# Attention on one core: a new order of score matmuls with seven shared PSUM banks, and value columns split by query halves

## The chip, the cores and the metric

The kernel runs on 1 core of one Trainium2 chip. The metric is the device time of one execution in microseconds, and lower is better. A core has five engines that work at the same time: TensorE (PE, with its weight loads shown as PEld), VectorE (DVE), ScalarE (ACT), GpSimd (POOL), and SyncE (SP), which issues the transfers. PE writes to PSUM alone, which has eight banks of 128 partitions by 512 fp32 values. DVE and ACT read results out of it. GpSimd works on SBUF.

## The reference

There are four layers over a sequence of 2048 rows of width 576. Layers 1 and 3 (called A) are attention with 32 heads of 18 columns, layers 2 and 4 (called B) have one key and value head for all 32 query heads.

```python
def _A_ref(x, wqkv, wo):
    ...
    scores = jnp.einsum("bhqd,bhkd->bhqk", q, k) * (Dh ** -0.5)
    p = _softmax(scores, axis=-1)
    o = jnp.einsum("bhqk,bhkd->bhqd", p, v)
    ...
x = x + _A_ref(_layernorm(x, axis=-1), A_wqkv, A_wo)
x = x + _B_ref(_layernorm(x, axis=-1), B_wq, B_wk, B_wv, B_wo)
x = x + _A_ref(_layernorm(x, axis=-1), A_wqkv, A_wo)
x = x + _B_ref(_layernorm(x, axis=-1), B_wq, B_wk, B_wv, B_wo)
```

Everything is fp32. Softmax takes the maximum of each row of scores, the exponentials of scores less that maximum, and their sum.

## The kernel before

A layer has a stretch of projections (layer norm, transposes, queries, keys and values) and then its attention. The output projection of a layer runs into the projections of the next. Attention is cut into 64 **units**: 16 pairs of heads (`p`) by 4 blocks of 512 queries (`u`). The loop over units is at line 908.

In a unit three kinds of work are mixed.

- **Maxima** (`max_mm`, line 581). Queries stand on PSUM's partitions and keys in columns: 16 score tiles of 128 queries by 512 keys for each head `a` of the pair. PE computes a tile (L613), DVE takes the maximum of each row (L620). When 32 are done, `max_final` (L759) folds them, GpSimd splits the result in two parts (`hl`), DVE transposes it (L768), and it goes through DRAM into two rows of `big`. From then on a matmul with the queries subtracts the maximum by itself. Maxima run 14 steps ahead of the exponentials, and a unit has 8 steps.
- **Exponentials** (`exp_mm`, line 776). Keys stand on partitions and queries in columns: 16 tiles of 128 keys by 512 queries for each head. PE computes the tile (L782), ACT writes its exponential to a tile `pt` (L791); every fifth goes to a slot of the tile `side` instead.
- **Value columns** (`pv_block`, line 804). PE multiplies values, 18 columns and one of ones, by the exponentials, and adds up in the one bank `oacc` (L812). Four matmuls stand side by side on PE, each on its own 32 of oacc's partitions: two heads by even and odd chunks of 128 keys. So a unit has 8 blocks of 512 columns, each four matmuls wide, and at its end ACT copies oacc to a slot of `side` (L200, called at line 818). `o_sum` (line 821) adds the odd half to the even one on GpSimd, two copies of 32x512 and an addition. Then the row of sums goes through DRAM to be inverted (`l_part`, `l_inv`, `l_out`, `l_rows`), GpSimd multiplies by it (`o_mul`), and `o_out` stores the block. Value columns lag 1152 columns behind (`LAG`).

Score tiles of the two heads go in pairs: one takes the upper half of PE's rows and the other the lower, so both run at once.

A **shared pair** of maxima moves work from DVE to ACT. For two key blocks of the same queries, a tile `d` (L605) is the score of the difference of the two key blocks; ACT takes its relu (L610) to a slot of `side`. The tile `t` (L613) is the score of the second block, and one DVE instruction (L617) adds the relu and takes the maximum. Since max(a, b) = b + relu(a - b), DVE has one pass for two tiles.

The order of a unit is written out in the table `UNIT` (line 67). Each word is one pair of score tiles, a letter for each head: `e` an exponential, `m` a maximum, `d` and `t` the halves of a shared pair. A number after a word says how many value columns follow. PE goes through the words and numbers as they stand. The other engines read tiles in the order in which PE wrote them. A unit before has 4 `d` and 4 `t`, 24 `m` and 32 `e`.

PSUM's eight banks are oacc, three banks for `m` and `t` (`mtile`, line 186) and four for `e` and `d` (`etile`, line 189), each set taken in turn.

The table `UNIT` is used by units 0 to 61 of a layer. In the last two no maxima are left or few, and `ENDS` and `LAST` take its place.

## Time and profile before

| | |
|---|---|
| median of 3 runs | 5597.66 us |
| lowest and highest | 5596.14 and 5599.7 us |
| span of the profiled execution | 5596.1 us |
| its own time | 5596.14 us, the lowest of the three |
| PE, DVE, ACT, POOL busy | 5580.9, 4941.3, 4934.9, 1755.0 us |
| granted TensorE clock, mean | 0.999 |

The profile is one execution. A page gives busy time by engine, the chain of work that ended last, and groups of instructions by line, with their count, their busy time, the mean length of one in ns, and the idle time of the engine before them with what ended it. The times of single instructions come from the timeline, and busy time in a stretch from the view by stretch. Matmuls overlap, and so do instructions of DVE and ACT that follow each other: the rate of an engine is read from the distance between starts and not from the length of one. An fp32 matmul of value columns is recorded as two, so four matmuls side by side are eight records.

### The profile page before, as it was taken

The page shows a single profiled execution, that of the slowest core. Times are in us where ns is not written, and L with a number is a line of the kernel's source. Part 1 is how long each engine was busy: PE and PEld are TensorE (multiplying, and loading weights), DVE is VectorE, ACT ScalarE, POOL GpSimd, SP SyncE. Part 2 cuts the span into 40 slices and gives each one's busy share as a digit, 9 for nine tenths or more (in the row PEclk, how much of TensorE's full clock was granted, in tenths as well). Part 3 has the DMA queues.
Part 4 walks back from the last instruction along what each step waited for, and adds up shares of the span by engine and source line. Part 5 has one row for each costly group of instructions (what it writes and reads, how often), then busy time and mean ns, then how long its engine had stood idle before and what let it go on. Part 6 is the DMA issues. An engine that isn't in the chain of part 4 may idle for free.

```text
span 5596.1 us, 137398 instructions
## 1 busy us (share of the span) xinstructions
PE 5580.9 (100%) x53372; PEld 2836.4 (51%) x53372; DVE 4941.3 (88%) x9504; ACT 4934.9 (88%) x9884; POOL 1755.0 (31%) x2245
## 2 busy tenths in 40 slices
PE   9999999999999999999999999999999999999999
PEld 8644444444844444444686444444448444444446
DVE  5799999998699999999747999999977999999995
ACT  3599999999299999999626999999992999999996
POOL 3133333334233323333421433333342333333332
PEclk9999999999999999999999999999999999999999
DMA  7311111111420110101253111111114201010002
GB/s 238 109 51 35 40 36 40 36 38 29 131 63 24 24 24 21 24 20 25 61 197 97 49 40 35 39 37 37 37 34 137 53 24 24 24 24 20 24 14 80
DMA packets 259573, 293.56 MB, mean 52 GB/s; under 512 B 133724, under 2 KB 173916, under 8 KB 249200
## 3 DMA queue, kind: packets, MB, share of 16 engines
q1 hardware_dynamic: 258920, 284.78, 18.0%
q8 instruction: 419, 6.86, 0.5%
q14 instruction: 234, 1.92, 0.1%
HBM read 158.77 MB, written 121.95 MB: 50 GB/s over the span
## 4 chain that ended last, share of the span: by engine, by line
PE 99%; DVE 1%; ACT 0%; DMA 0%; issue 0%; POOL 0%; SPq 0%; ACTq 0%; POOLq 0%
PE oacc L812 39%; PE pse L782 23%; PE psm L613 21%; PE psn L280 6%; PE psq L439 6%; PE psd L605 3%; PE ps L272 0%; DVE mx L620 0%; PE oacc L273 0%; POOL big L229 0%; DVE ev L456 0%; DMA raw<-in_A_wqkv_dram 0%; DMA kd<-kd_d 0%; ACT ev L447 0%; ACT evr L453 0%
## 5 line engine op out<-in xcount | busy, mean ns | idle before, releaser
L620 DVE TENSOR_REDUCE mxd<-psm 128x1 f32<-128x512 f32 x5952 | 3746.8, 682 | 181.0 <-PE psd L605 66.3
L791 ACT ACTIVATE pt<-pse 128x512 f32<-128x512 f32 x6584 | 3573.3, 627 | 26.1 <-PE pse L782 1.2
L613 PE MATMUL psm<-big 62*128 62x512 f32 x7200 | 2505.5, 444 | 0.7
L782 PE MATMUL pse<-big 64*128 64x512 f32 x8192 | 2415.3, 431 | 1.5 <-ACT evr L453 1.5
L812 PE MATMUL oacc<-pt,vbuf 128*19 128x192 f32 (+6 forms) x20244 | 1795.2, 379 | 0.0
L782 PEld LDWEIGHTS pse<-big 64*128 64x128 f32 x8192 | 1212.9, 184 | 890.9 <-ACT pt L791 513.9
L613 PEld LDWEIGHTS psm<-big 62*128 62x128 f32 x7200 | 1132.8, 184 | 677.2 <-DVE mxd L620 259.6
L812 PE MATMUL oacc<-side,vbuf 128*19 128x64 f32 (+6 forms) x5004 | 1402.3, 377 | 0.0
L791 ACT ACTIVATE side<-pse 128x512 f32<-128x512 f32 x1608 | 995.4, 619 | 5.9
L202 POOL TENSOR_SCALAR hl<-neg 128x8 fp32r<-128x8 f32 x256 | 50.9, 199 | 2446.1 <-DVE neg L759 2446.1
L812 PEld LDWEIGHTS oacc<-pt,vbuf 128*19 128x19 f32 x20244 | 447.8, 97 | 601.6 <-issue 485.2
L617 DVE CUSTOM_DVE_ANT_0 side<-psm,side 128x512 f32<-128x512 f32 x992 | 679.6, 685 | 37.5 <-PE psm L613 14.0
L835 POOL TENSOR_TENSOR rl<-lt,mone 128x8 f32<-128x8 f32 x256 | 423.5, 1654 | 662.0 <-DMA lt<-os 653.9
L610 ACT ACTIVATE side<-psd 128x512 f32<-128x512 f32 x992 | 598.1, 644 | 3.5 <-PE psd L605 3.5
L812 PE MATMUL oacc<-pt,vy 128*19 128x384 f32 (+2 forms) x5700 | 587.2, 417 | 0.0
L812 PE MATMUL oacc<-side,vy 128*19 128x384 f32 (+2 forms) x1404 | 455.6, 415 | 0.0
L605 PE MATMUL psd<-kd,big 54*128 54x512 f32 x992 | 428.4, 473 | 0.8 <-DMA kd<-kd_d 0.8
L812 PEld LDWEIGHTS oacc<-side,vbuf 128*19 128x19 f32 x5004 | 317.3, 97 | 147.0 <-issue 119.5
L447 ACT ACTIVATE ev<-psq 128x512 fp32r<-128x512 f32 (+1 forms) x112 | 67.0, 598 | 315.8 <-PE psq L439 274.2
L848 POOL TENSOR_TENSOR os<-os,rb 96x512 f32<-96x512 f32 x256 | 328.7, 1284 | 21.6 <-DMA rb<-r_d 21.6
L826 POOL TENSOR_TENSOR os<-os,side 96x512 f32<-96x512 f32 x240 | 307.5, 1281 | 20.0
L202 POOL TENSOR_SCALAR os<-side 32x512 f32<-32x512 f32 x480 | 294.5, 614 | 40.1 <-POOL hl L763 0.4
(93 smaller groups left out, 3314.2 us busy)
## 6 DMA issues: line engine op xcount, KB each, us to landing
big<-qk_d SPq DMA_DIRECT2D x180, 432.0 KB
qk_d<-ev SPq DMA_DIRECT2D x96, 512.0 KB
qk_d<-ev SPq DMA_DIRECT2D x120, 256.0 KB
rb<-r_d SPq DMA_DIRECT2D x512, 36.0 KB
o_d<-os SPq DMA_DIRECT2D x512, 36.0 KB
o<-o_d SPq DMA_DIRECT2D x64, 256.0 KB
big<-m_d SPq DMA_DIRECT2D x512, 4.0 KB
lt<-os SPq DMA_DIRECT2D x512, 2.0 KB
```

Source lines behind the costliest of these rows:

```text
L202: eng.tensor_scalar(dst, src, 1.0, 0.0, op0=OP.mult, op1=OP.add)
L280: nc.tensor.matmul(ps, lhs[:, xc, :], wsm[:, wc, h * 288:(h + 1) * 288], start=i == 0, stop=i == len(TERMS) - 1)
L439: nc.tensor.matmul(ps[:n].rearrange("p (u t) -> p u t", u=2)[:, us], w[:, wc, :n], xts[T][:, us, xc, :], start=(xc, wc) == TERMS[0], stop= ...
L605: nc.tensor.matmul(ps, q[b:b + 3 * DH, c0:c0 + P], kds[p if is_a else 0][b:b + 3 * DH], start=True, stop=True)
L610: nc.scalar.activation(r, ps, AF.Relu)
L613: nc.tensor.matmul(ps, q[b:b + KM, c0:c0 + P], k[b:b + KM, kb * 512:(kb + 1) * 512], start=True, stop=True)
L617: nc.vector.tensor_tensor_reduce(out=r, in0=ps, in1=r, scale=1.0, scalar=-3.0e38, op0=OP.add, op1=OP.max, accum_out=mx[:, r0:r0 + 1])
L620: nc.vector.reduce_max(mx[:, r0:r0 + 1], ps, axis=AX.X)
L782: nc.tensor.matmul(e, k[r:r + KE, kc * P:(kc + 1) * P], q[r:r + KE, u * 512:(u + 1) * 512], start=True, stop=True)
L791: nc.scalar.activation(pt, e, AF.Exp, scale=SCALE)
L812: nc.tensor.matmul(oacc[j:j + DH + 1, cs], v_of(kc)[:, 2 * p + a if is_a else 0, :], pts[p, u, i][:, cs], start=kc < 2 and c0 == 0, stop=k ...
L835: nc.gpsimd.tensor_tensor(rl, lts.pop((p, u)), mone, op=OP.pow)
```

## The change

It has four parts.

1. A new table `UNIT`: 11 groups of value columns in place of 12, and three shared pairs a unit in place of four (3 `d`, 3 `t`, 26 `m`, 32 `e`). The cut for the last units moves with it (`CUT_AT`).
2. Seven banks for all score tiles. A second table `BANKS` says for each tile which bank it takes, as a rank by age: 0 is the bank that was taken longest ago, 2 the third oldest. Outside of the units the sets of four and three stay.
3. The four matmuls side by side are now two heads by two halves of the 512 queries, over the same chunk of keys. A unit's value work is 16 blocks of 256 columns, and oacc uses 256 columns of its bank. oacc is copied out as 128x256, GpSimd copies that on to `sums` instead of adding halves, and multiplies 128x256. The transfers of `l_part`, `l_rows` and `o_out` are four in place of two, each half as long.
4. `pt` tiles have 17 buffers in place of 15, and four slots of `side` in place of three take exponentials.

```diff
-UNIT = """te ee 256 em me 384 et em me 512 et me ee 448 md dm em 384 em me 192 me ee me 192 md em 384
-          me me em 384 em ee te 192 mm ee 384 dm em em 384 me"""
+UNIT = """ee 384 em ee mm 384 em mm ee 384 me te ee 512 me me em 320 em me 192 me ed dm 448 em em me
+          320 me em te 256 ee de mt 512 em mm ee 384 em mm"""
+
+BANKS = """01 00 02 01 00 00 10 00 02 20 01 01 10 00 01 00
+           00 01 01 00 01 00 00 01 01 00 01 00 02 01 00 02"""
-CUT_AT = 10
+CUT_AT = 9
...
+    order = list(range(7))
+    turns = {"e": [0, 1, 2, 3], "m": [4, 5, 6]}
+
+    def bank(b, name):
+        order.remove(b)
+        order.append(b)
+        return psum.tile([P, 512], F32, tag=f"b{b}", bufs=1, name=name)
+
+    def oldest(rank):
+        return lambda name: bank(order[rank], name)
...
-        return pool.tile(list(shape), dt, tag="p", bufs=15, name=name)
+        return pool.tile(list(shape), dt, tag="p", bufs=17, name=name)
...
-                n, c0 = divmod(pv_at[0], 512)
-                w = min(cols, 512 - c0)
+                n, c0 = divmod(pv_at[0], 256)
+                w = min(cols, 256 - c0)
...
-            for i in range(i, i + 4) if turn[0] % 2 else range(i + 3, i - 1, -1):
-                a, kc = (i // 2) % 2, i // 4 * 2 + i % 2
-                j = 64 * a + 32 * (kc % 2)
-                nc.tensor.matmul(oacc[j:j + DH + 1, cs], v_of(kc)[:, 2 * p + a if is_a else 0, :], pts[p, u, i][:, cs],
-                                 start=kc < 2 and c0 == 0, stop=kc >= 14 and c1 == 512)
+            for i in range(4) if turn[0] % 2 else range(3, -1, -1):
+                a, h = divmod(i, 2)
+                nc.tensor.matmul(oacc[32 * i:32 * i + DH + 1, c0:c1], v_of(kc)[:, 2 * p + a if is_a else 0, :],
+                                 pts[p, u, a, kc][:, 256 * h + c0:256 * h + c1],
+                                 start=kc == 0 and c0 == 0, stop=kc == NCH - 1 and c1 == 256)
...
+                    copy(nc.scalar if m_done[0] < 4 * ns else nc.vector, oc, oacc[:, :256])
...
-            for j in (0, 64):
-                copy(nc.gpsimd, t[j:j + 32], oc[j + 32:j + 64])
-            nc.gpsimd.tensor_tensor(t[:96], t[:96], oc[:96], op=OP.add)
+            copy(nc.gpsimd, sums[u % 2], ocs.pop((p, u)))
...
-            for a in range(2):
-                nc.sync.dma_start(lt[64 * a:64 * a + 64, :], sums[u % 2][64 * a + DH:64 * a + DH + 1, :])
+            for i in range(4):
+                nc.sync.dma_start(lt[32 * i:32 * i + 32, :], sums[u % 2][32 * i + DH:32 * i + DH + 1, :])
...
+                    take = oldest(BANKS[i][a] if more_m or m_done[0] < 4 * ns else 0)
                     if kinds[a] == "e":
-                        exp_mm(p, u, n // 2 * 4 + 2 * a + n % 2, mtile if m_done[0] == 4 * ns and n_e % 7 % 2 else etile)
+                        exp_mm(p, u, a, e_next[a], take)
```

What this makes of PE's order is seen about the end of a unit's value columns, where oacc is copied out (the third group of a table ends there), in the first layer. Before, PE has these rows; `oacc` are value columns, `pse` tiles for exponentials and `psm` tiles for maxima:

```order
L812 MATMUL oacc<-side,vy 19x512
L812 MATMUL oacc<-pt,vy 19x512 x3
L782 MATMUL pse<-big 128x512
L613 MATMUL psm<-big 128x512 x2
L782 MATMUL pse<-big 128x512 x3
L812 MATMUL oacc<-pt,vbuf 19x448 x4
```

And after the change, at the same place:

```order
L829 MATMUL oacc<-pt,vy 19x128 x2
L829 MATMUL oacc<-side,vy 19x128 x2
L829 MATMUL oacc<-pt,vy 19x256 x4
L633 MATMUL psm<-big 128x512
L801 MATMUL pse<-big 128x512
L633 MATMUL psm<-big 128x512
L801 MATMUL pse<-big 128x512 x3
L829 MATMUL oacc<-side,vbuf 19x256 x2
L829 MATMUL oacc<-pt,vbuf 19x256 x6
```

A value group is now cut at every 256 columns, so 384 columns are 128 and 256, and 512 are two pieces; three pairs of score tiles stand between groups here in both.

DVE's rows of a whole unit before, from the end of one set of maxima (`neg`) to the next; L617 is the sum and maximum of a shared pair, recorded as two instructions, and L768 the transpose:

```order
L620 TENSOR_REDUCE mxd_97<-psm 128x1 x6
L768 STREAM_TRANSPOSE tr<-hl_102 128x32
L620 TENSOR_REDUCE mxd_97<-psm 128x1 x7
L617 ISA side,mxd_97<-psm,side 128x512
L617 ISA mxd_97 128x1
L620 TENSOR_REDUCE mxd_97<-psm 128x1 x6
L617 ISA side,mxd_97<-psm,side 128x512
L617 ISA mxd_97 128x1
L620 TENSOR_REDUCE mxd_97<-psm 128x1 x2
```

And after:

```order
L640 TENSOR_REDUCE mxd_99<-psm 128x1 x4
L788 STREAM_TRANSPOSE tr<-hl_102 128x32
L640 TENSOR_REDUCE mxd_99<-psm 128x1 x8
L637 ISA side,mxd_99<-psm,side 128x512
L637 ISA mxd_99 128x1
L640 TENSOR_REDUCE mxd_99<-psm 128x1
L637 ISA side,mxd_99<-psm,side 128x512
L637 ISA mxd_99 128x1
L640 TENSOR_REDUCE mxd_99<-psm 128x1 x13
```

The rows before are cut where two more L617 and three more reductions follow; after, one more L617 follows and the set ends. The transpose stands four reductions behind `neg` and not six.

More of the change, by code (lines that the diff above doesn't have):

```diff
@@ L86 @@
 UNIT, LAST = slots(UNIT), slots(LAST)
+BANKS = [[int(x) for x in w] for w in BANKS.split()]
+assert len(BANKS) == len(UNIT)
 KINDS = [[w[a] for w, _ in UNIT if w[a] != "e"] for a in range(2)]
@@ L172, in tile_kernel @@
     kd_d = dram.tile([D, 3, 512], F32, name="kd_d")
-    rb = cst.tile([P, 512], F32, name="rb")
+    rb = cst.tile([P, 256], F32, name="rb")
+    sums = [cst.tile([P, 256], F32, name=f"os{i}") for i in range(2)]
     mxd = [cst.tile([P, 32], F32, name=f"mxd{i}") for i in range(2)]
@@ L177, in tile_kernel, with turn_of @@
         nc.gpsimd.memset(t, -3.0e38)
[L179 removed]
     hls = [cst.tile([P, 32], F32R, name=f"hl{i}") for i in range(2)]
[L182 removed]
+    for t in [rb] + [h_.bitcast(F32) for h_ in hls]:
         nc.gpsimd.memset(t, 0.0)
+    order = list(range(7))
[6 more added lines that the diff above has]
+        return lambda name: bank(order[rank], name)
+    def turn_of(kind, name):
+        b = turns[kind].pop(0)
+        turns[kind].append(b)
+        return bank(b, name)
     def mtile(name):
[L187 removed]
+        return turn_of("m", name)
     def etile(name):
[L190 removed]
+        return turn_of("e", name)
     def ptile(name, shape=(P, 512), dt=F32):
[L193 removed]
+        return pool.tile(list(shape), dt, tag="p", bufs=17, name=name)
     def xtile(name, shape=(P, 2, 9, 256), dt=F32R):
@@ L603, in max_mm @@
             if kind == "d":
-                ps = etile("psd")
+                ps = tile("psd")
                 nc.tensor.matmul(ps, q[b:b + 3 * DH, c0:c0 + P], kds[p if is_a else 0][b:b + 3 * DH],
```

52 lines of the change are left out of this document (22 added, 30 removed).

## The prediction

> **What bounds the kernel now.** First the page: which engine is full, and what its chain of waits ends in.
>
> ```profile
> PE 5580.9 (100%) x53372; PEld 2836.4 (51%) x53372; DVE 4941.3 (88%) x9504; ACT 4934.9 (88%) x9884; POOL 1755.0 (31%) x2245
> PE 99%; DVE 1%; ACT 0%; DMA 0%; issue 0%; POOL 0%; SPq 0%; ACTq 0%; POOLq 0%
> ```
>
> PE is named for all the span. But matmuls overlap in these rows, so a wait of some 0.1 us can't be seen in busy time. Hence the view by stretch, over a stretch of the first layer, with the groups of instructions of the same stretch (of ACT's copies out of oacc and of DVE's rows).
>
> ```profile
> 401.88:1297.60 895.72, 895.72 (x9216) 403.62 (x9216) 852.68 (x1633) 889.80 (x1776) 285.50 (x352) 1.00 0.15 37
> L200 ACT ACTIVATE side<-oacc 128x512 f32<-128x512 f32 x48 | 28.7, 598 | 0.0
> L620 DVE TENSOR_REDUCE mxd<-psm 128x1 f32<-128x512 f32 x1153 | 726.0, 682 | 34.1 <-PE psd L605 11.4 <-PE psm L613 9.4 <-PE pse L782 4.2
> L617 DVE CUSTOM_DVE_ANT_0 side<-psm,side 128x512 f32<-128x512 f32 x192 | 131.5, 685 | 7.3 <-PE psm L613 2.5 <-PE pse L782 0.2
> ```
>
> The columns of the first row are length, then busy time of PE, PEld, DVE, ACT and POOL. oacc is copied out once a unit, so 48 units took 895.72 us: 18.66 us a unit, at a granted clock of 1.00. Of this DVE shows 17.76 busy and ACT 18.54. To see what PE needs, I read its timeline in one unit (start, length, line).
>
> ```profile
> 402.12 0.72 PE L613 MATMUL psm<-big 62*128 62x512 f32 x2
> 402.46 0.63 PE L782 MATMUL pse<-big 64*128 64x512 f32 x3
> 403.01 0.95 PE L812 MATMUL oacc<-pt,vbuf 128*19 128x448 f32 x8
> 403.89 0.49 PE L613 MATMUL psm<-big 62*128 62x512 f32 x1
> ...
> 404.87 0.56 PE L812 MATMUL oacc<-pt,vbuf 128*19 128x64 f32 x9
> ...
> 405.64 0.49 PE L782 MATMUL pse<-big 64*128 64x512 f32 x1
> ...
> 406.30 0.34 PE L812 MATMUL oacc<-pt,vbuf 128*19 128x192 f32 x1
> ...
> 406.75 0.50 PE L613 MATMUL psm<-big 62*128 62x512 f32 x1
> ...
> 407.80 0.35 PE L812 MATMUL oacc<-pt,vbuf 128*19 128x192 f32 x2
> ...
> 409.69 0.50 PE L613 MATMUL psm<-big 62*128 62x512 f32 x1
> ...
> 410.59 0.50 PE L812 MATMUL oacc<-pt,vbuf 128*19 128x384 f32 x1
> ...
> 411.36 0.50 PE L782 MATMUL pse<-big 64*128 64x512 f32 x1
> ```
>
> PE alternates between score pairs and a group of value columns. Three pairs last 0.89 (402.12 to 403.01) or 0.90 (409.69 to 410.59), two pairs 0.66 (405.64 to 406.30): a third pair adds 0.24, so opening a group is dear. 448 value columns last 0.88 (403.01 to 403.89), 192 last 0.45 (406.30 to 406.75): 1.68 ns a column and 0.13 to get back to scores. The old table has 12 groups, eight of three pairs and four of two: 8 x 0.90 + 4 x 0.66 + 12 x 0.13 + 4096 x 0.00168 = 7.20 + 2.64 + 1.56 + 6.88 = 18.28 us. The unit took 18.66, so PE waits 0.38 us a unit, in places such as 403.89 to 404.87 (0.98 for three pairs) and 406.75 to 407.80 (1.05). What it waits for, in the view of waits for this stretch:
>
> ```profile
> PEld pse L782 <- ACT pt L791: 91.2, 154, 0.8
> PEld psm L613 <- DVE mxd L620: 49.0, 144, 0.6
> ```
>
> These are waits for a bank to be read out; most lie under running matmuls. The other two engines have their own floors:
>
> ```profile
> 404.42 3.68 DVE L620 TENSOR_REDUCE mxd<-psm 128x1 f32<-128x512 f32 x6 [0.22 <-PE psd L605]
> 408.02 0.20 DVE L768 STREAM_TRANSPOSE tr<-hl 128x32 f32<-128x32 f32 x1
> 408.15 4.56 DVE L620 TENSOR_REDUCE mxd<-psm 128x1 f32<-128x512 f32 x7
> 412.62 0.68 DVE L617 CUSTOM_DVE_ANT_0 side<-psm,side 128x512 f32<-128x512 f32 x1
> ...
> 413.31 1.29 DVE L620 TENSOR_REDUCE mxd<-psm 128x1 f32<-128x512 f32 x2
> ...
> 421.35 0.69 DVE L617 CUSTOM_DVE_ANT_0 side<-psm,side 128x512 f32<-128x512 f32 x1
> ...
> 421.96 0.69 DVE L620 TENSOR_REDUCE mxd<-psm 128x1 f32<-128x512 f32 x1
> 422.68 0.19 DVE L759 TENSOR_REDUCE neg<-mxd 128x8 f32<-128x32 f32 x1
> 402.31 0.60 ACT L200 ACTIVATE side<-oacc 128x512 f32<-128x512 f32 x1
> 402.81 0.59 ACT L791 ACTIVATE pt<-pse 128x512 f32<-128x512 f32 x1
> 412.87 2.07 ACT L791 ACTIVATE pt<-pse 128x512 f32<-128x512 f32 x4
> 414.78 0.65 ACT L610 ACTIVATE side<-psd 128x512 f32<-128x512 f32 x1
> ```
>
> A reduction behind another costs DVE 0.60 (404.42 to 408.02, six). A sum-and-maximum of a shared pair (L617) costs 0.61 (421.35 to 421.96) to 0.69 (412.62 to 413.31), say 0.65. Transpose and final maximum add 0.13 (408.02 to 408.15) and about 0.31 (421.96 to 422.68 in place of 0.60, and 0.19). So DVE needs 24 x 0.60 + 4 x 0.65 + 0.44 = 17.44 us a unit. ACT needs 0.48 an exponential or relu (412.87 to 414.78, four), and 0.50 for the copy of oacc: 36 x 0.48 + 0.50 = 17.78. PE is the bound by 0.5, and the other two are close.
>
> By the Trainium skill (Perfetto Trace Analysis, "Identifying the Most-Contended Engine") the occupancy of Vector and Scalar is a fair measure of how near they are to their limit, by which ACT with 99.3% would be the bound. This trace speaks against it: ACT's rows overlap, 0.6 long but 0.48 apart.
>
> **The change, part by part.** *Fewer switches on PE.* The new table has 11 groups, ten of three pairs and one of two, and the same 32 pairs and 4096 columns: 10 x 0.90 + 0.66 + 11 x 0.13 + 6.88 = 17.97. That is 0.31 us a unit less.
>
> *Blocks of 256 columns.* Cut at every 256, a unit's value work falls into 20 pieces in place of 16. 384 columns in one piece last 0.77 (410.59 to 411.36), in pieces of 64 and 320 also 0.77 (404.87 to 405.64): a piece costs nothing to the 0.01 that these rows resolve, so 0 to 0.04 us a unit; I take 0. That the two halves of a query block stream out of the same tile has no row of its own; the two maxima at 402.12 read one tile, big, side by side and lose nothing, so 0 again.
>
> The far bound is that a matmul's fixed part is not hidden. In the same stretch, 64 and 128 columns:
>
> ```profile
> L812 PE MATMUL oacc<-pt,vbuf 128*19 128x64 f32 x920 | 43.4, 224 | 0.0
> L812 PE MATMUL oacc<-pt,vy 128*19 128x128 f32 x922 | 49.4, 275 | 0.0
> ```
>
> 64 columns more cost 51 ns, so 224 - 51 = 173 ns of a record don't depend on columns. A piece is two passes of four matmuls side by side; bare, four more pieces would cost 4 x 2 x 0.173 = 1.38 us a unit. The two rows of 0.77 say that it is hidden.
>
> The Trainium skill (TensorEngine Tiling (Array Packing), "Instruction Overhead") speaks against this part: each matmul carries an overhead of about 60 cycles, and a dimension that is small already shouldn't be cut. With the 2.4 GHz that the skill gives for TensorE (Trainium Kernel Development and Optimization, "NeuronCore Architecture") an estimate is 25 ns for each of 4 x 2 passes, 0.2 us a unit, or four times that if the four matmuls of a pass queue; the unit would be 18.5 to 19.1. This trace does not show such a cost at 64 columns.
>
> *Three shared pairs.* A shared pair is two maxima for one relu on ACT and one pass on DVE. One pair fewer: ACT loses a relu, 0.48. DVE has 26 reductions and 3 sums in place of 24 and 4, 2 x 0.60 - 0.65 = 0.55 more: 17.99 a unit. DVE's floor is now as high as PE's.
>
> *Copy of half a bank.* ACT copies 256 columns of oacc, not 512. No row has that copy from PSUM; it saves at least nothing and at most the 0.50; I take 0.25, by the half. ACT then needs 17.78 - 0.48 - 0.25 = 17.05 and drops out as a bound.
>
> *GpSimd.* The add of two halves goes: two copies of 32x512 and the add become one copy. POOL has time to spare, and only the lt chain waits on it:
>
> ```profile
> 407.49 1.29 POOL L848 TENSOR_TENSOR os<-os,rb 96x512 f32<-96x512 f32 x1
> 411.46 1.65 POOL L835 TENSOR_TENSOR rl<-lt,mone 128x8 f32<-128x8 f32 x1 [2.68 <-DMA lt<-os]
> 422.96 0.20 POOL L202 TENSOR_SCALAR hl<-neg 128x8 fp32r<-128x8 f32 x1 [9.85 <-DVE neg L759]
> ```
>
> POOL stands idle 9.85 us before the next unit's hl, so this is worth 0; without that cover the 1.3 us of a copy or product would delay hl, and with it DVE's transpose four reductions (2.4 us) behind. The three steps over SP (lt, rb, o_d) issue four transfers each, not two: six more a unit in SP's queue, ahead of the rows for later units. Waiting for POOL they hold SP no longer than now, since POOL's copy is shorter; DMA is busy 0.15 of this stretch; 0.
>
> *Seven banks by rank.* This is the term with no row. Now each maximum's matmul has to wait until all but two of DVE's earlier tiles are read, each exponential's and relu's until all but three of ACT's are. Counted through the new ranks, of the 29 banks that a unit takes over from DVE, 18 allow three or four tiles behind, ten allow two and one allows one; of the 35 from ACT, 6 allow four, 17 three and 12 two. So DVE may carry about one tile (0.60 us) more over a long value group, which is where it runs dry. On the other hand a late DVE now also holds up exponentials. Bounds: the waits vanish, and the unit is DVE's 17.99; or DVE keeps the idle time it has before its rows now, (34.1 + 7.3) / 48 = 0.86, and the unit is 18.85. The nearest row is PE's own wait of 0.38 over its floor; with both floors at 17.97 and 17.99 and a deeper queue I take 0.35: a unit of 18.32.
>
> *Sum.* 18.32 - 18.66 = -0.34 us a unit, times 62 units a layer that use the table, times 4: -84 us. The last two units of a layer are bound by exponentials alone and projections are untouched: 0. The two more pt buffers can free at most small waits of the projections, 0 taken. The profiled execution has a span of 5596.1 us, which is also the fastest time of the three; from the median 5597.66 the sum gives 5513 us.
>
> **Rivals.**
> *DVE runs dry* (slower). With 29 passes DVE has only 18.66 - 17.99 = 0.67 us of idle time a unit before the kernel is slower than now. Place: the two value groups of 512 and the one of 448, where DVE gets two tiles (1.2 us) for 1.8 to 1.9 us of PE work. For it: the 0.86 of idle time now. At 18.85 a unit: +0.19 x 248 = +47, 5645 us. Against it: ranks that allow three behind.
> *Order gives it back.* The banks' ranks tie ACT's and DVE's tiles together, and waits grow by the 0.31 that was saved: within 11 us of now, 5598.
> *Waits vanish.* DVE's 17.99 holds: -0.67 x 248 = -166, 5432 us.
> *Short matmuls cost* (slower from a point on). If a quarter of the 1.38 us is bare, 0.34, the gain is gone, 5598; all of it gives 5513 + 1.38 x 248 = 5855 us. The rows of 0.77 are against it. The tiling page's overhead, above, would be this rival's mechanism.
> *That PE's saving isn't real* (the third pair no cheaper in the new groups) is part of the second.
>
> **How the numbers follow.** Chances: forecast (unit 18.2 to 18.5, so 5484 to 5558) 0.58; waits vanish 0.10; between forecast and no change 0.05; no change 0.07; DVE runs dry 0.17; short matmuls past zero 0.03. So faster by over 0.2% (11 us, about what a measurement of this kernel can tell from no change) 0.73, same 0.07, slower 0.20. The range leaves out the far end of both outer rivals: 5440 to 5625.
>
> **What would show it.** Right: about 18.3 us a unit between copies of oacc, three pairs still 0.90 to value columns, 256-wide pieces at 0.43 each, DVE's idle time before its reductions under 0.4 a unit, ACT's share down by some 0.7 us a unit. Wrong: PE's three pairs at 1.0 or more in most groups (banks), DVE rows with idle time behind the groups of 448 and 512 columns (dry), or value groups longer than 1.68 ns a column (pieces).

## The result and the profile after

The changed kernel takes 5567.22 us (median of 4 runs, 5565.1 to 5567.69) against 5597.17 for the kernel before (4 runs beside it, 5596.14 to 5599.7): a ratio of 0.9945, with a 95% interval of 0.993 to 0.9959. It is faster by 30 us. The forecast was 84 us faster. The direction was right, and the size was off by more than half.

First the page: its busy times, and the row of the chain by engine.

```profile
PE 5542.7 (100%) x61788; PEld 3174.4 (57%) x61788; DVE 4992.7 (90%) x9504; ACT 4806.7 (86%) x9636; POOL 1070.9 (19%) x1731
PE 22%; ACT 1%; DVE 0%; issue 0%; ACTq 0%
```

PE is still full in this view; ACT has lost 2 points of the span and DVE gained 2. The chain by engine adds up to 23% of the span here, where before it covered all of it, so nothing is read from it. Then the same stretch of the first layer as in the prediction, by stretch and by group (columns as there), and the first and the last of the copies out of oacc in it, from ACT's timeline (start, length, line).

```profile
401.88:1297.60 895.72, 895.72 (x10848) 471.08 (x10852) 871.56 (x1647) 872.76 (x1744) 159.59 (x260) 1.00 0.15 38
L640 DVE TENSOR_REDUCE mxd<-psm 128x1 f32<-128x512 f32 x1259 | 773.5, 682 | 22.5 <-PE psm L633 18.2 <-PE pse L801 3.1
L810 ACT ACTIVATE pt<-pse 128x512 f32<-128x512 f32 x1239 | 674.7, 614 | 19.4 <-PE psm L633 6.9 <-PE pse L801 2.1 <-ACT pt L810 0.4
L220 ACT ACTIVATE side<-oacc 128x256 f32<-128x256 f32 x49 | 19.4, 395 | 0.1
```
```profile
402.09 0.40 ACT L220 ACTIVATE side<-oacc 128x256 f32<-128x256 f32 x1
...
1290.34 0.40 ACT L220 ACTIVATE side<-oacc 128x256 f32<-128x256 f32 x1
```

49 copies are 48 units: (1290.34 - 402.09) / 48 = 18.51 us a unit, where 18.32 was forecast and 18.66 was measured before. 0.15 us times 248 units is 37 us, of which 30 arrive. ACT's rows of these copies in all four layers show the rest: from the first to the last one of a layer, 59 units, the four layers together save 35.5 us, and what lies outside of these stretches is 4.5 us longer (1193.2 us against 1188.7).

PE's timeline in a unit after the change, in the part that turned out to matter:

```profile
406.37 0.50 PE L633 MATMUL psm<-big 62*128 62x512 f32 x1
...
407.40 0.40 PE L829 MATMUL oacc<-pt,vbuf 128*19 128x256 f32 x2
...
408.27 0.49 PE L801 MATMUL pse<-big 64*128 64x512 f32 x1
...
408.84 0.40 PE L801 MATMUL pse<-big 64*128 64x512 f32 x1
409.17 0.51 PE L829 MATMUL oacc<-pt,vbuf 128*19 128x64 f32 x10
...
409.84 0.50 PE L633 MATMUL psm<-big 62*128 62x512 f32 x1
409.84 0.73 PE L801 MATMUL pse<-big 64*128 64x512 f32 x2
410.18 0.63 PE L633 MATMUL psm<-big 62*128 62x512 f32 x2
410.53 0.50 PE L801 MATMUL pse<-big 64*128 64x512 f32 x1
410.95 0.63 PE L829 MATMUL oacc<-pt,vbuf 128*19 128x256 f32 x8
411.51 0.50 PE L801 MATMUL pse<-big 64*128 64x512 f32 x2
```

Three pairs that wait for nothing last 0.90 (408.27 to 409.17), as before. Ahead of the group of 448 they last 1.03 (406.37 to 407.40), and ahead of the group of 256 columns 1.11 (409.84 to 410.95). In the second case the last tile of the third pair, an exponential, starts late, at 410.53. What it waited for is seen on ACT's timeline at that place, in a stretch that holds one instruction:

```profile
409.82 0.66 ACT L810 ACTIVATE pt<-pse 128x512 f32<-128x512 f32 x1
```

It ends at 409.82 + 0.66 = 410.48, and PE starts 0.05 later. The tile that took the bank before was one of ACT's.

Since `BANKS` fixes which tile had a bank before, this can be followed for every tile: the start of its matmul in PE's timeline against the end of the instruction that last read its bank. Over 47 units from 401.88 on, the late tile ahead of the group of 256 starts 0.05 behind the end of an instruction of ACT in all 47, and the last tile ahead of the group of 448 does so in 41. Where the first group of 384 is late in this way (14 units), the bank is ACT's too. In none of these cases had another of the seven banks come free earlier, so no other rank would have shortened these waits at their places.

Over the 48 units the three pairs ahead of the group of 256 last 0.24 more than 0.90, and those ahead of the group of 448 last 0.09 more (means of the timeline's starts over this stretch; the other waits in this text are worked out the same way). Two groups of 384 have 0.07 and 0.05, and the groups of 512 have 0.03 and 0.02. Together with small rests this is 0.55 us of waits a unit (the unit of 18.51 less PE's floor of 17.96, see below; with 0.90 and 0.66 taken off for the pairs it is 0.53), where the forecast had 0.35. By the same count the old order has 0.41.

The view of waits says something else. It names DVE for most of PE's waiting:

```profile
PEld pse L801 <- DVE mxd L640: 84.4, 232, 0.4
PEld psm L633 <- DVE mxd L640: 58.9, 164, 0.4
PEld pse L801 <- ACT pt L810: 18.9, 101, 0.3
```

Most of this lies under running matmuls, and an entry goes to the semaphore that came last. So who sets the unit was left to experiments.

### The profile page after: what moved, and what is told of

It is laid out like the page before. It is cut to its first block, busy times and chain, and to the rows that moved or that the text cites. A ratio compares the mean times of both kernels' runs of the same rounds, so it can differ in the third digit from the quotient of the medians.

```text
span 5565.1 us, 157695 instructions
## 1 busy us (share of the span) xinstructions
PE 5542.7 (100%) x61788; PEld 3174.4 (57%) x61788; DVE 4992.7 (90%) x9504; ACT 4806.7 (86%) x9636; POOL 1070.9 (19%) x1731
## 5 line engine op out<-in xcount | busy, mean ns | idle before, releaser
L640 DVE TENSOR_REDUCE mxd<-psm 128x1 f32<-128x512 f32 x6448 | 3961.0, 682 | 117.5 <-PE psm L633 95.7
L633 PE MATMUL psm<-big 62*128 62x512 f32 x7448 | 2255.5, 434 | 1.3 <-ACT pt L810 0.5
L829 PE MATMUL oacc<-pt,vbuf 128*19 128x256 f32 (+2 forms) x24544 | 1742.6, 341 | 0.0
L801 PEld LDWEIGHTS pse<-big 64*128 64x128 f32 x8192 | 1188.7, 184 | 714.4 <-DVE mxd L640 425.5
L829 PEld LDWEIGHTS oacc<-pt,vbuf 128*19 128x19 f32 x24544 | 628.1, 98 | 659.0 <-issue 428.6
L829 PE MATMUL oacc<-side,vbuf 128*19 128x256 f32 (+3 forms) x6016 | 774.1, 341 | 0.0
L829 PE MATMUL oacc<-pt,vy 128*19 128x256 f32 (+1 forms) x8192 | 564.8, 341 | 0.0
L829 PEld LDWEIGHTS oacc<-pt,vy 128*19 128x19 f32 x8192 | 225.4, 98 | 194.5 <-issue 134.1
L829 PE MATMUL oacc<-side,vy 128*19 128x256 f32 (+1 forms) x2016 | 263.0, 339 | 0.0
L300 PE MATMUL psn<-wsm,ot 128*128 128x288 f32 x1792 | 244.8, 296 | 0.4
L300 PEld LDWEIGHTS psn<-wsm,ot 128*128 128x128 f32 x1792 | 238.6, 188 | 5.5 <-issue 3.0
```

Of the source, the lines that this page charges most:

```text
L300: nc.tensor.matmul(ps, lhs[:, xc, :], wsm[:, wc, h * 288:(h + 1) * 288], start=i == 0, stop=i == len(TERMS) - 1)
L633: nc.tensor.matmul(ps, q[b:b + KM, c0:c0 + P], k[b:b + KM, kb * 512:(kb + 1) * 512], start=True, stop=True)
L640: nc.vector.reduce_max(mx[:, r0:r0 + 1], ps, axis=AX.X)
L801: nc.tensor.matmul(e, k[r:r + KE, kc * P:(kc + 1) * P], q[r:r + KE, u * 512:(u + 1) * 512], start=True, stop=True)
L829: nc.tensor.matmul(oacc[32 * i:32 * i + DH + 1, c0:c1], v_of(kc)[:, 2 * p + a if is_a else 0, :], pts[p, u, a, kc][:, 256 * h + c0:256 * h ...
```

## The experiments

Five theories were tested. **D**: DVE, whose floor rose to 17.99, sets the unit. **B**: the order in which banks are given out does. **A**: ACT does, because the banks that it reads come free late. **P**: PE itself needs that long for a third pair. **S**, a form of A that came up later: ACT's sum over a unit counts, wherever its work stands. "A unit" below is the mean of 56 units in the middle of the first layer. Ratios are to the kernel before.

**d1: shorter maxima.** DVE gets relief and nobody else. The reductions of the units that share the banks read 448 of 512 keys; the kernel leaves the other 64 out of these maxima.

```diff
-                    nc.vector.reduce_max(mx[:, r0:r0 + 1], ps, axis=AX.X)
+                    nc.vector.reduce_max(mx[:, r0:r0 + 1], ps[:, :448] if shared else ps, axis=AX.X)
```

> The changed kernel, whose reductions of plain maxima read 448 of 512 columns (64 columns are left out of those maxima). Theory D (DVE sets the unit: its floor of 17.9 to 18.0 us and two places a unit where it runs dry make 18.51): with 26 reductions some 0.06 us shorter DVE's floor falls by about 1.6 us, DVE no longer binds, and the unit falls to PE's floor plus small waits, 18.0 to 18.2 us, 5470 to 5490 us in all. Theory B (the shared banks' ranks tie exponentials to banks, whatever DVE's speed): the unit stays at 18.4 to 18.5, 5545 to 5567 us.

5566.03 us, 0.9946 (0.9934 to 0.9959), a unit of 18.50: no change, as was expected of theory B. The stretch and DVE's group in it:

```profile
401.88:1297.60 895.72, 895.72 (x10852) 472.31 (x10850) 805.21 (x1647) 872.97 (x1745) 159.67 (x260) 1.00 0.15 38
L640 DVE TENSOR_REDUCE mxd<-psm 128x1 f32<-128x448 f32 x1259 | 706.7, 617 | 88.7 <-PE psm L633 61.7 <-PE pse L801 23.4
```

DVE's busy time fell from 871.56 to 805.21, and all of it became idle time of DVE (22.5 to 88.7). The waits of PE stayed at the same places. Theory D falls.

**k0 and k1: other ways to give out banks.** k0 sets every rank to 0, so that each tile takes the bank that was taken longest ago. k1 keeps the new table with the old split of four banks and three.

```diff
-BANKS = """01 00 02 01 00 00 10 00 02 20 01 01 10 00 01 00
-           00 01 01 00 01 00 00 01 01 00 01 00 02 01 00 02"""
+BANKS = "00 " * 32
```
```diff
-                    take = oldest(BANKS[i][a] if more_m or m_done[0] < 4 * ns else 0)
+                    own = "m" if kinds[a] in "mt" else "e"
+                    take = (lambda name, own=own: turn_of(own, name)) if more_m or m_done[0] < 4 * ns else oldest(0)
```

> The changed kernel with every rank 0, so that each score tile takes the bank that was taken longest ago. Theory D: the number of banks counts and the ranks hardly, 0 to +25 us against the changed kernel (5567 to 5592). Theory B: the ranks matter, over 30 us either way.

> The changed kernel with the old split of banks in the units: three in turn for m and t, four in turn for e and d. Theory D: DVE may then carry only two tiles behind, runs dry longer behind the groups of 448 and 512 columns, and the unit goes to 18.8 to 19.0 us, 70 to 120 us over the changed kernel (5637 to 5687). Theory B: exponentials no longer wait for banks that DVE holds, and the kernel gets faster, below 5550 us.

k0: 6016.19 us, 1.0749 (1.0734 to 1.0764), a unit of 20.31. k1: 5896.0 us, 1.0535 (1.052 to 1.0549), a unit of 19.82. The new table needs its ranks; without them it would have lost 5 to 7%. Other ways to give out the banks cost 1.3 to 1.8 us a unit, far outside of what the prediction had as bounds for this term. k0 meets what was expected of theory B, k1 meets neither expectation. At the late tiles of k0 the bank that is taken is in no unit the first to come free: another had been free for 0.34 to 0.90 us in the mean, place by place. In the changed kernel the late tiles already take the first bank to come free, so wrong ranks there are not what its 0.55 comes from; whether a wholly other table of ranks would do better, no run shows.

**p1 and s1: the parts without the new table.** p1 is the kernel before with the value columns by query halves, the half copy, GpSimd's single copy, four transfers and 17 buffers, in the old order and with split banks; its edit on the kernel before, cut to its core:

```diff
-                n, c0 = divmod(pv_at[0], 512)
+                n, c0 = divmod(pv_at[0], 256)
...
-                copy(nc.scalar if m_done[0] < 4 * ns else nc.vector, oc, oacc)
+                    copy(nc.scalar if m_done[0] < 4 * ns else nc.vector, oc, oacc[:, :256])
```

s1 is the kernel before with seven shared banks and ranks that fit its own order, and nothing else:

```diff
+                    take = oldest(BANKS[i][a] if more_m or m_done[0] < 4 * ns else 0)
...
-                        max_mm(a, mtile)
+                        max_mm(a, take)
```

> The kernel before with the layout of value columns alone changed: two heads by two query halves, half a bank copied out, the copy on GpSimd, the four transfers, 17 buffers; the old table of the unit and the old split of banks. Both theories: PE is still the bound with 12 groups, four more pieces cost at most 0.02 us a unit, ACT's shorter copy frees 0.2 us where ACT's banks are waited for: 5575 to 5600 us.

> The kernel before with the seven banks shared by rank, the ranks chosen for the old table so that each tile takes the bank whose reader ends first; table, value columns and four shared pairs as before. Theory A: a tile no longer waits for its own kind's bank, the waits of 0.38 us a unit shrink by 0.1 to 0.25, 5535 to 5575 us. Theory P: the waits stay, 5590 to 5605 us.

p1: 5598.97 us, 1.0002 (0.9993 to 1.0011), a unit of 18.63. s1: 5609.41 us, 1.0023 (1.0014 to 1.0032), a unit of 18.68. Neither gains. For s1 that is a miss of theory A, which had 5535 to 5575 us. The banks of the kernel before, followed as above, show why: its largest wait, 0.14 ahead of the second group of 192 columns, already stands on a bank of ACT's that was the first of the seven to come free, in all 47 units. So the gain comes with the new table, for which the ranks are a condition. PE's floor (18.26 before, 17.96 after) points at the table's 11 groups; no run parts them from its three shared pairs.

**x1 and x2: shorter exponentials.** x1 relieves ACT as d1 relieved DVE. x2 has both. These kernels leave out the last 64 of the 512 columns of each exponential; the value columns of the second query half are read 64 further left instead, so that PE has as much work as before.

```diff
-            nc.scalar.activation(pt, e, AF.Exp, scale=SCALE)
+            nc.scalar.activation(pt[:, :448], e[:, :448], AF.Exp, scale=SCALE)
...
-                                 pts[p, u, a, kc][:, 256 * h + c0:256 * h + c1],
+                                 pts[p, u, a, kc][:, 192 * h + c0:192 * h + c1],
```

> The changed kernel, whose exponentials read and write 448 of 512 columns (the last 64 are left out, and value columns of the second query half read 64 columns further left instead). DVE is as it was. Theory A (at the third pair of a group all seven banks are taken and the first to come free is one that ACT reads; ACT's lateness there makes PE's waits of 0.51 us a unit): ACT needs 32 x 0.05 us less a unit, the waits shrink by 0.25 us or more, 18.1 to 18.25 us a unit, 5475 to 5510 us. Theory P (the waits are PE's own, from weights that load late behind any wait, whatever the reader does): unchanged, 5555 to 5575 us.

> The same with the reductions of plain maxima over 448 columns as well. Theory A, and DVE as the next to bind: near PE's floor, 18.0 to 18.1 us a unit, 5440 to 5470 us, clearly below the run with short exponentials alone. If DVE has no part at all: the same as that run. Theory P: unchanged, 5555 to 5575 us.

x1: 5506.6 us, 0.9839 (0.9825 to 0.9852), a unit of 18.31, which is 0.20 less than the changed kernel. x2: 5453.03 us, 0.9744 (0.9731 to 0.9757), a unit of 18.11. The stretch and ACT's group in x1:

```profile
401.88:1297.60 895.72, 895.72 (x10962) 457.59 (x10959) 879.29 (x1665) 824.34 (x1762) 161.63 (x261) 1.00 0.15 38
L810 ACT ACTIVATE pt<-pse 128x448 f32<-128x448 f32 x1253 | 626.0, 549 | 58.9 <-PE psm L633 24.4 <-PE pse L801 16.7 <-ACT pt L810 0.5
```

Relief of ACT shortens the unit where relief of DVE did nothing; once ACT is relieved, relief of DVE brings 0.20 more. So ACT binds first and DVE next. The banks say the same: the late tiles that are left in x1 stand ahead of the two groups of 512 and start behind an instruction of DVE, in 45 and in 46 of 47 units. With both relieved the unit is within 0.15 of PE's floor of 17.96. Theory P, by which the waits are PE's own, falls too: PE's work was not touched.

**z1: the same in the old order.** p1 with short exponentials, and value columns read as in x1.

```diff
-            nc.scalar.activation(pt, e, AF.Exp, scale=SCALE)
+            nc.scalar.activation(pt[:, :448], e[:, :448], AF.Exp, scale=SCALE)
```

> p1 (the order and the split banks of before, with the new value columns and copies; 5599 us), with each exponential over 448 of 512 columns, and the value columns of the second half read 64 columns further left, so that part of the exponentials is left out. Theory A for the old order too (its 0.38 us of waits in a unit come from ACT, which is at 17.78 us of 18.66): the waits shrink by 0.25 to 0.35 us, 5515 to 5545 us. If they are PE's own cost or DVE's: 5590 to 5605 us.

5558.21 us, 0.9928 (0.9916 to 0.9941), a unit of 18.52: 0.11 less than p1, 41 us. This is between the two expectations. Part of the old order's waits were ACT's as well, but less than in the new order.

**v1 and v2: one `d` and one `t` moved.** A relu tile (`d`) moves from row 16 to the end of the table, and a `t` from row 26 to row 5, to thin out ACT's tiles in the second half of the unit. v1 keeps the ranks, v2 fits them to v1's trace.

```diff
-UNIT = """ee 384 em ee mm 384 em mm ee 384 me te ee 512 me me em 320 em me 192 me ed dm 448 em em me
-          320 me em te 256 ee de mt 512 em mm ee 384 em mm"""
+UNIT = """ee 384 em ee mm 384 em mt ee 384 me te ee 512 me me em 320 em me 192 me em dm 448 em em me
+          320 me em te 256 ee de mm 512 em mm ee 384 em md"""
```

> The changed kernel with one relu tile (d) moved from the group before the 448 columns to a group of the other part of the table, and its t with it; ranks untouched. Theory A: ACT has one tile less in the four groups in which it is full, the waits before the groups of 448 and 256 columns shrink, 5530 to 5560 us, unless the old ranks no longer fit and cost more than that. Theory P: 5555 to 5575 us.

> v1 (5792 us) moved one d from slot 16 to slot 31 and one t from slot 26 to slot 5, and kept the ranks that fitted the old places. Here the ranks are fitted to the moved table: each take gets the bank that came free first in v1's own trace. If v1's loss came from its ranks, nearly all of it goes: a unit of 18.4 to 18.6 us and 5535 to 5575 us. If the loss came from moving the two exponentials, the time stays over 5700 us.

v1: 5792.39 us, 1.035 (1.0336 to 1.0364), a unit of 19.43. v2: 5718.85 us, 1.0215 (1.0201 to 1.0229), a unit of 19.09, with waits of 0.46 ahead of the second group of 384, the one behind the moved `d`, and 0.30 ahead of the second group of 512. By its number v2 falls to the second half of its expectation, by which the move itself costs. Its banks speak against that: at both places the bank that is taken is in none of 47 units the first to come free, and another had been free for 0.49 and 0.20 us in the mean. Ranks taken from the trace of a kernel with bad ranks are not yet good ones. What the move costs with ranks that fit, no run shows. (The recorded text speaks of two exponentials; what moves is a relu and a maximum.)

**c1 and c2: value columns moved.** c1 gives 64 columns of a group of 512 to the group ahead of the wait of 0.24; c2 does the same for the wait of 0.09 as well.

```diff
-          320 me em te 256 ee de mt 512 em mm ee 384 em mm"""
+          384 me em te 256 ee de mt 448 em mm ee 384 em mm"""
```

> The changed kernel, with 64 value columns moved from the second group of 512 (448 are left) to the group of 320 two rows earlier (384 now). The columns of a unit, the groups, the kinds and the ranks stay. Theory A (ACT is full in the middle of the unit, and the banks that it reads come free late): PE comes 0.11 us later to the slots from 23 on, where it waits 0.24 us on a bank of ACT's, so that this wait shrinks by about 0.1 us, and the unit with it, if what follows can use it: 5537 to 5565 us. Theory P (the waits are PE's own cost of a third pair): no change, 5563 to 5571 us.

> c1, and 64 value columns moved too from the first group of 512 (448 are left) to the group of 192 (256 now), just ahead of the group in which the changed kernel waits 0.09 us on a bank of ACT's. Theory A: both waits shrink, the unit comes to 18.3 to 18.4 us, 5515 to 5550 us. Theory P: no change, 5563 to 5571 us.

c1: 5567.4 us, 0.9946 (0.9933 to 0.9958), a unit of 18.50: no change, which is the number that theory P had, though the wait did shrink as theory A had it. PE's timeline of c1 at that place:

```profile
410.42 0.73 PE L801 MATMUL pse<-big 64*128 64x512 f32 x2
...
411.01 0.49 PE L801 MATMUL pse<-big 64*128 64x512 f32 x1
411.99 0.50 PE L801 MATMUL pse<-big 64*128 64x512 f32 x2
```

The late exponential now starts 0.59 after the first pair (410.42 to 411.01), and not 0.69 (409.84 to 410.53 above). In the mean the wait ahead of the group of 256 fell from 0.24 to 0.12, and the one ahead of the next group rose from 0.03 to 0.14. It moved one group on, and both late tiles stand on banks of ACT's that were the first to come free, in all 47 units. PE was held off a little longer, but ACT didn't get through its tiles sooner. c2: 5584.63 us, 0.9974 (0.9964 to 0.9984), a unit of 18.58, slower than the changed kernel. There the wait ahead of the group of 448 went (0.09 to 0.01), but the group before it, of 192 columns and now of 256, got one of 0.09, the wait ahead of the old group of 256 grew back (0.12 to 0.21), and two groups of 384 have 0.03 and 0.05 more. In both misses the waits moved to neighbouring groups: ACT's lateness in this part of the unit is a debt that is passed on.

**x3 and x4: where relief counts.** Short exponentials in the crowded rows alone, and in all others alone; `row` is the tile's row of the table, and value columns are read as in x1.

```diff
-            nc.scalar.activation(pt, e, AF.Exp, scale=SCALE)
+            w = 448 if 12 < row < 26 else 512
+            nc.scalar.activation(pt[:, :w], e[:, :w], AF.Exp, scale=SCALE)
```
```diff
+            w = 448 if 0 <= row < 13 or row > 25 else 512
```

> x1 (all exponentials over 448 of 512 columns, 5506.6 us) with the short form in rows 13 to 25 of the table alone: 13 of the 32 exponentials of a unit, in the stretch from the pairs ahead of the group of 192 value columns to those of the second group of 512, where 16 of ACT's 35 tiles stand in five groups. The value columns of the second half are read 64 further left, so part of the exponentials is left out. Theory A, crowded stretch: the waits of 0.09, 0.24 and 0.03 us in there go for the most part, and the unit with them: 18.2 to 18.35 us, 5507 to 5530 us. Theory S (ACT's sum counts, wherever it is relieved): 13/32 of what x1 gained, -25 us, 5535 to 5550 us.

> The other half of x1: the short form in rows 0 to 12 and 26 to 31 alone, 19 of the 32 exponentials of a unit; the same part of the exponentials' columns is left out of the values. Theory A, crowded stretch: only the waits of 0.07 and 0.05 us ahead of two groups of 384 can go, and ACT enters the crowded stretch no earlier, since it has caught up by then: 5535 to 5565 us, less gained than in x3. Theory S: 19/32 of what x1 gained, -36 us, 5524 to 5538 us, more than in x3.

x3: 5519.92 us, 0.9862 (0.9849 to 0.9876), a unit of 18.33. x4: 5548.67 us, 0.9915 (0.9901 to 0.9928), a unit of 18.45. 13 short exponentials in the crowded rows gain 0.17 us a unit, nearly all of x1's 0.20. 19 short ones elsewhere gain 0.06. Both times lie in the ranges of theory A and outside of those of S, which had x4 ahead of x3. This decides against S. (The rows from 7 to 12, ahead of the crowded ones, and 7 of the 19 exponentials with them, belong to x4.) PE's timeline of x3 at the groups of 256 and 512:

```profile
407.85 0.49 PE L633 MATMUL psm<-big 62*128 62x512 f32 x1
...
408.81 0.63 PE L830 MATMUL oacc<-pt,vbuf 128*19 128x256 f32 x8
409.37 0.73 PE L801 MATMUL pse<-big 64*128 64x512 f32 x3
...
410.43 0.63 PE L830 MATMUL oacc<-pt,vy 128*19 128x256 f32 x8
```

The three pairs ahead of the group of 256 last 0.96 (407.85 to 408.81) and not 1.11; in the mean their wait is down from 0.24 to 0.05. Those ahead of the group of 512 now last 1.06 (409.37 to 410.43): their wait rose from 0.03 to 0.14, on a bank that DVE read (46 of 47 units). In x4 the waits ahead of the two groups of 384 are gone, but the one ahead of the group of 256 stays (0.26), so what ACT gains elsewhere does not reach it. Part of x4's relief is lost to DVE: ahead of the first group of 512 the wait rose from 0.03 to 0.11, on a bank that DVE read (45 of 47).

**y1 and y2: the copy of oacc.** y1 lets ACT do its copy twice, y2 gives it to DVE.

```diff
-                    copy(nc.scalar if m_done[0] < 4 * ns else nc.vector, oc, oacc[:, :256])
+                    for _ in range(2 if m_done[0] < 4 * ns else 1):
+                        copy(nc.scalar if m_done[0] < 4 * ns else nc.vector, oc, oacc[:, :256])
```
```diff
+                    copy(nc.vector, oc, oacc[:, :256])
```

> The changed kernel, with ACT's copy of oacc done twice, one behind the other, so that ACT has about 0.3 us more in a unit and stands at 17.35 us of 18.51, still under PE's floor of 17.96. Theory A: ACT's lateness is passed on to the banks, the unit grows by 0.1 to 0.3 us, 5590 to 5640 us. By the prediction's reading (an engine below PE's floor is no bound): no change, 5561 to 5573 us.

> The changed kernel, with DVE copying oacc in the units in which ACT did it: ACT has 0.27 us less (16.8 us a unit), DVE about 0.35 us more (18.35 us a unit, by the rows of 29 passes and a copy). Theory A: ACT's relief comes through only as far as DVE lets it; DVE then becomes the bound with 18.4 to 18.6 us, 5540 to 5590 us. If DVE is as near to its limit as the rows say, and every late pass counts: 18.6 to 18.8 us, 5590 to 5640 us.

y1: 5661.14 us, 1.0114 (1.0101 to 1.0128), a unit of 18.90. y2: 5674.36 us, 1.0139 (1.0123 to 1.0154), a unit of 18.95. Both are slower than expected, for a reason that neither theory had. PE's timeline of y1 behind the copy, then ACT's:

```profile
404.94 0.64 PE L801 MATMUL pse<-big 64*128 64x512 f32 x3
405.77 0.63 PE L829 MATMUL oacc<-pt,vbuf 128*19 128x256 f32 x8 [0.19 <-ACT side L220]
```
```profile
404.90 0.82 ACT L220 ACTIVATE side<-oacc 128x256 f32<-128x256 f32 x2
```

The next value group waits for the copy itself (ACT ends at 404.90 + 0.82 = 405.72, PE starts at 405.77). The wait at this place is 0.26 in y1 and 0.48 in y2, where the changed kernel has 0.03: that is 0.23 of y1's 0.39 us a unit, and all of y2's 0.44. So these runs don't tell what ACT's load does. They show that one copy of half a bank on ACT fits under three pairs, and two don't.

**w1 and w2: added work that nobody waits for.** Two small copies on ACT, inside the crowded rows and outside.

```diff
+                if more_m and i == 19:
+                    nc.scalar.activation(junk, junk, AF.Copy)
+                    nc.scalar.activation(junk, junk, AF.Copy)
```
```diff
+                if more_m and i == 3:
```

> The changed kernel, with two small copies more on ACT (128x32, of a tile that nothing else uses) in each unit, behind row 19 of the table, in the crowded stretch. ACT copies of 128 and 256 columns last 0.29 and 0.40 us, so one of 32 should last about 0.20 and hold ACT for about 0.1: 0.2 us a unit. No other engine waits for them. ACT would stand at 17.25 of PE's floor of 17.96. Theory A, crowded stretch: they come out whole, as 0.1 to 0.25 us a unit, 5590 to 5630 us. Theory S (only ACT's sum counts): the same as in w2. By the prediction's reading (ACT is under PE's floor and no bound): 5562 to 5573 us.

> The same two copies behind row 3 of the table, outside the crowded stretch, where three groups of 384 value columns have three of ACT's tiles each. Theory A, crowded stretch: ACT has room there and takes them in, 0 to 0.06 us a unit, 5562 to 5582 us. Theory S: as much as in w1.

w1: 5633.83 us, 1.0065 (1.0053 to 1.0078), a unit of 18.79. w2: 5599.62 us, 1.0006 (0.9997 to 1.0015), a unit of 18.64. PE's and ACT's timelines in w1, at the place of the wait of 0.24 (lines stand two further down here):

```profile
411.18 0.50 PE L635 MATMUL psm<-big 62*128 62x512 f32 x1
411.19 0.73 PE L803 MATMUL pse<-big 64*128 64x512 f32 x2
411.53 0.63 PE L635 MATMUL psm<-big 62*128 62x512 f32 x2
412.27 0.50 PE L803 MATMUL pse<-big 64*128 64x512 f32 x1
412.70 0.41 PE L831 MATMUL oacc<-pt,vbuf 128*19 128x256 f32 x4
```
```profile
410.72 0.64 ACT L812 ACTIVATE pt<-pse 128x512 f32<-128x512 f32 x1
411.20 0.27 ACT L940 ACTIVATE junk<-junk 128x32 f32<-128x32 f32 x1
411.50 0.23 ACT L941 ACTIVATE junk<-junk 128x32 f32<-128x32 f32 x1
411.64 1.55 ACT L812 ACTIVATE pt<-pse 128x512 f32<-128x512 f32 x3
```

The two copies put the next exponential off to 411.64, 0.92 behind the one at 410.72, where 0.48 is usual: they cost 0.44, not the 0.2 that was expected. The three pairs now last 1.52 (411.18 to 412.70). Of the 0.44, 0.29 come out in the unit. In w2 the copies cost 0.41, and 0.14 come out, ahead of the first group of 512, which is the next place with four of ACT's tiles; 0 to 0.06 were expected, so w2 is a miss. Both runs also upset the ranks, which had been fitted without the copies. At the late tile of w2 another bank had been free for 0.18 us in the mean, in all 47 units, and at that of w1 for 0.14. So w2's 0.14 may be due to its ranks alone, and up to half of w1's 0.29. What is left of w1's, 0.15 or more, is a cost though ACT's sum is 17.05 + 0.44 = 17.5 and so far under PE's floor of 17.96: the prediction's reading falls with w1, while w2 leaves it open.

**What the runs show together.** ACT's work can be set against PE's group by group. A tile holds ACT for 0.478 (starts of exponentials behind each other), and PE's time for three pairs and a value group is 0.90 and the length of the group, so 1.89 for 512 columns, 1.78 for 448, 1.67 for 384, 1.57 for 320, 1.46 for 256, and 1.12 for 192 with two pairs. From the first group of 512 to the second stand seven groups with 23 of ACT's tiles and the copy: 23 x 0.478 + 0.27 = 11.26 us of ACT in 1.89 + 1.57 + 1.12 + 1.78 + 1.57 + 1.46 + 1.89 = 11.28 us of PE. The other four groups, all of 384, have 12 tiles: 5.74 in 6.68. By this count nearly all the room that ACT has in a unit, 0.94 us, stands in those four groups. It can't be saved up: ACT can't read tiles that PE hasn't made, and PE is at most seven banks ahead. The count doesn't say which of the seven groups are the tight ones; x3 and x4 put them in the last five.

## Why the prediction was right or wrong

*Fewer switches on PE*: right. Three undisturbed pairs still last 0.90 and two 0.66; the floors counted from the timelines are 18.26 before and 17.96 after, against 18.28 and 17.97.

*Blocks of 256 columns at no cost*: right. Groups of 384 columns last 0.777 after and 0.772 before, and those of 512 last 0.990 and 0.985: 0.005 us a piece more, 0.02 a unit. By the Trainium skill (TensorEngine Tiling (Array Packing), "Instruction Overhead") some 60 cycles a matmul should have shown, 0.2 us a unit by the prediction's estimate; this trace has a tenth of that, and p1, which has the pieces without the new order, is at 1.0002.

*Three shared pairs*: the sum was right, and DVE's 17.99 was no bound yet (d1). It is the next one, as x2 shows.

*Copy of half a bank*: right in size. ACT's timeline of the changed kernel at one copy:

```profile
420.86 0.39 ACT L220 ACTIVATE side<-oacc 128x256 f32<-128x256 f32 x1
421.12 2.09 ACT L810 ACTIVATE pt<-pse 128x512 f32<-128x512 f32 x4
```

It holds ACT for 0.26 to 0.27 (420.86 to 421.12), not 0.50. What the prediction didn't see is that PE's next value group depends on it (y1).

*GpSimd and transfers at 0*: right. POOL's busy time fell from 285.50 to 159.59, and p1 is unchanged.

*Seven banks by rank, waits of 0.35*: **this is the step that failed**. The waits are 0.55. The term was taken from the nearest row, the old waits of 0.38, with the reason that both floors were under 18; and the end of the term on the copy, by which ACT's sum is 17.05 "and drops out as a bound", is where it went wrong. ACT's 17.05 is right as a sum over a unit. But ACT has no room in seven of the 11 groups, and the banks can't save up for it: the late tiles of the two longest waits, 0.24 and 0.09, stood on banks that ACT had yet to read, with no other bank free. With waits of 0.55 the prediction's own sum gives 17.97 + 0.55 = 18.52.

*The rivals.* The unit of 18.51 lies just past the upper end of the forecast, 18.5, in the band between forecast and no change, which had a chance of 0.05. "Order gives it back" comes nearest: waits grew, but by 0.14 of the 0.31 that it named. None of the rivals was ACT. "DVE runs dry" has the rows that it asked for, as here in DVE's timeline behind the group of 448 (idle time in brackets), and d1 shows that they cost nothing.

```profile
408.83 3.08 DVE L640 TENSOR_REDUCE mxd<-psm 128x1 f32<-128x512 f32 x5 [0.24 <-PE psm L633]
```

*What would show it.* The sign named for a failure was PE's three pairs at 1.0 or more in most groups. It stood in two of 11, ahead of 448 and 256 columns, and that was enough for 0.33 of the 0.55. Two signs of being right failed as well. DVE's idle time before its reductions is 22.5 / 48 = 0.47 us a unit, and not under 0.4. ACT's busy time fell by 0.36 a unit (889.80 to 872.76 in the stretch), and not by 0.7: exponentials that do not follow each other count with their full 0.6 there, and not with 0.478.

## What to carry to other kernels

An engine whose sum over a period is under the bound's is not thereby out of the way: compare the two sums within each stretch that the buffers between them can't bridge, here a few groups of seven banks. Whether an engine binds was told here by a small relief of it alone, at two places, and by following each late tile's bank to the instruction that read it last; the sum of waits pointed at the wrong engine. Added work told less, since it upset the ranks too. A table of banks belongs to one order of work, and a move of score tiles in that order needs a new one.

## What the runs showed of the hardware

- A matmul started about 0.05 us after the end of the instruction that read its bank (410.48 to 410.53; in w1 the end of the exponential at 411.64, 412.22, to 412.27).
- A wait costs PE some 0.1 us beyond itself. From the last tile of a pair to the value columns it takes 0.33 in a group that doesn't wait (408.84 to 409.17) and 0.42 in one that does (410.53 to 410.95). In these rows the late matmul itself is 0.50 long and not 0.40, as the first ones behind a value group are. In the means over 47 units it is 0.43 against 0.33 from the last tile to the value columns, and 0.50 against 0.39 for the matmul. No run shows why.
- Two ACT copies of 128x32 out of SBUF, each 0.23 to 0.27 long, cost 0.41 to 0.44 between exponentials, nearly as much as an exponential of 512 columns (0.478).
- The view of waits named DVE for 143 us of PE's waiting in the stretch. d1 took DVE's part down (84.4 and 58.9 us to 74.7 and 17.2, in the rows below), and the time did not move.

```profile
PEld pse L801 <- DVE mxd L640: 74.7, 189, 0.4
...
PEld psm L633 <- DVE mxd L640: 17.2, 41, 0.4
```
